# A retention layer with a GELU feed-forward layer on one core: the steps behind the 540th in another order, some of them on other engines

## The chip, the cores and the metric

The kernel runs on one core of a Trainium2 chip. Five engines work side by side: TensorE (PE in the profile; its weight loads PEld) multiplies matrices, VectorE (DVE), ScalarE (ACT) and GpSimd (POOL) work on elements, and SyncE (SP) issues DMA transfers. Each engine runs its own instructions in the order in which the program gives them, and waits for the others by semaphores. The metric is the device time of one execution in microseconds (us).

## The reference

```python
scores = scale * np.matmul(q, k.transpose(0, 1, 3, 2))      # q, k, v: 8 x 8 heads x 576 x 64
gamma = 1.0 - 2.0 ** (-5.0 - np.arange(H, dtype=np.float32))
Dmat = np.where(rel >= 0, gamma[:, None, None] ** rel[None, :, :], 0.0)
ret = scores * Dmat[None, :, :, :]
x = np.matmul(ret, v)                                       # then (b, s, h * d): 4608 x 512
h = x @ w_in                                                # 512 x 2048
g = 0.5 * h * (1.0 + np.tanh(c * (h + 0.044715 * h * h * h)))
out = g @ w_out                                             # 2048 x 512
```

Scores are decayed by the distance of two positions, with no softmax, so that the sum over earlier positions can be carried on as a state of 64 x 64 for each head.

## The kernel before

**Units and token blocks.** The 8 batches of 576 rows are cut into 40 units (u = 0 to 39), five for a batch: four of 128 rows and a tail of 64. The 4608 tokens of the second layer are cut into nine blocks (t = 0 to 8) of 512. The attention of a unit writes its columns of `xT`, a ring of three token blocks; a token block can begin when the units that cover it are done.

**The order is written out.** `ORDER` is a string of some 1370 steps. A loop at the end of the kernel takes them one by one and calls the function that the letter names; nothing reorders them later, so each engine's queue is the list, thinned to that engine's steps. Steps of different engines may overtake each other where their data allow. The last field of many steps names the engine: `v` VectorE, `a` ScalarE, `g` GpSimd; `q` without a letter is on VectorE.

**Steps of a unit u.** `L,u,n` loads q, k or v (n = 0, 1, 2) from SP into a page; a page is free again when the cast that reads it is done. `q,u` scales q by its decay to float16, `k,u` casts k, `v,u` scales v. `D,u` has a DMA on SP's queue transpose q and k. `B,u,w` is TensorE's work for the scores and the new state of unit u, and for the output of the unit before it, w (lines 550 to 595). `m,u` masks the scores, `a,u,h` adds to the state in float32 for either half h, `o` decays it, `z,u,h` makes its float16 copy in two instructions of 64 rows, and `x,u` moves the output into `xT`.

**Steps of a token block t.** Up to block 4 the first product is plain: `N,t,..` and `M` (line 790), with the gelu in `F` and `G`. For blocks 5 to 8 it is done with seven products of half size in place of eight: `s,t,i` makes four sums of blocks of `xT` (float16, in SBUF, in the area named `pages`), and `A,t,g,i` are the seven products of weight group g (line 1001). Their order in a group is 1, 6 and 2, 7 and 5, 4, 3: products 1, 6, 7 and 4 share one PSUM bank, 2, 5 and 3 the other, and `l,t,g,i` takes the partial results out (`l` 0 to 2 copy, 3 to 5 add). `f,t,g,i` is the gelu of a quarter. The second product is done in this way for most blocks: `H,t,pr,i` makes the sums of the gelu's output for a pair of 128 tokens (pr = 0 or 1; `ssum` in the profile, float16 in SBUF), `W,t,pr,i` are the seven products (line 904), and `V,t,pr,i` takes them out of PSUM into `u` and `ost`; `S,t,n` stores an `ost` from SP. `H,..,5` makes the two sums 1 and 3 in one instruction of 2048 columns, `H,..,1` and `H,..,3` make them one by one:

```python
if i == 5:
    a21, a11 = blk_a(t, pr, 1, 0), blk_a(t, pr, 0, 0)
    ...
    return combine(eng, s[4], a21.unsqueeze(1).to_broadcast([128, 2, HK, 128]), both, ALU.subtract)
```

All sums go through `combine` (line 850), copies and casts through `copy_on` (lines 284 and 286), the scalings of q and v through `times` (line 441):

```python
def combine(eng, out, a, b, op):
    (nc.vector if eng == "v" else nc.gpsimd).tensor_tensor(out=out, in0=a, in1=b, op=op)
```

**Buffers.** `ost` is a ring of four, so the `V` that begins the fifth waits for the store of the first; `qk16`, `v16` and the transposed `T` are rings of four units; `sz` (of `z`) is a ring of six. From unit 26 on nine pages are left for loads, since the sums of `w_in` and `xT` lie in the others. `i` and `j` steps cast a staged weight where there is one; here all weights are loaded and cast by DMAs on GpSimd's queue at the start, and these steps issue nothing.

Of the kernel before, what the change touches and what calls it, by code (L numbers as in the profile page):

```python
# [59 lines left out]
z,20,1,a B,21,20 F,3,14,1 F,3,2,1 L,26,0 N,4,4,0 a,21,0 L,24,1 W,3,1,1 m,21 U,3,0 V,3,0,0,a a,21,1  # L60
# [5 lines left out]
v,26,g V,3,1,3,a N,4,6,0 v,24,g k,27,a W,3,0,5 k,26,v z,23,1,g D,24 F,4,6,1 F,4,6,0 B,24,23 L,30,1
x,23 D,25 M,4,1 G,4,1 m,24 S,2,0 N,4,10,0 W,3,1,4 V,3,1,5,v B,25,24 D,26 W,3,0,2 a,25,0,g S,2,3
F,4,10,0 z,25,0,g V,3,0,4,v a,25,1 M,4,3 x,24 k,30,a W,3,0,3 D,27 G,4,3 m,25 H,4,0,5,v B,26,25
N,4,8,1 a,26,0 x,25 S,2,2 a,26,1 m,26 H,3,1,4,v v,27,g L,31,1 z,25,1,a F,4,8,1 k,31,a W,3,1,5
N,4,4,1 H,4,0,2,v z,26,0,g F,4,4,1 N,4,10,1 V,3,1,4,v B,27,26 N,4,14,1 L,28,0 W,3,1,3 V,3,0,6,v  # L70
L,29,0 L,28,1 o,26,1 x,26 s,5,1 F,4,10,1 V,3,0,2,a F,4,14,1 W,3,1,2 A,5,0,1 s,5,2 W,4,0,1 L,29,1
# [1047 lines left out]
```

## Time and profile before

| what | value |
|---|---|
| median of three runs | 294.59 us (294.44 to 296.1) |
| profiled execution, whole | 295.5 us |
| its span | 293.8 us |
| TensorE busy | 280.0 us (95%) |
| VectorE busy | 225.7 us (77%) |
| ScalarE busy | 166.6 us (57%) |
| GpSimd busy | 95.7 us (33%) |
| granted TensorE clock | 1.00 throughout |
| DMA | 49.77 MB, mean 169 GB/s |

The span is what the profiler saw of the one execution; 1.7 us lie around it. A row of a group gives the line, the engine, the operation, the tiles written and read, the shape, the count, the busy time in us with the mean of one in ns, and then the idle time of the engine ahead of it and what ended it. A row of the timeline gives start and duration in us, and in brackets the engine's idle time before. Rows of the trace are matched to steps by their order on each engine, which is the list's.

### The profile page before, as it was taken

What the parts mean: (1) busy time and instruction counts of PE and PEld (TensorE: products, weight loads), DVE (VectorE), ACT (ScalarE), POOL (GpSimd) and SP (SyncE); (2) the same over time, 40 slices, a digit from 0 to 9 for tenths busy, and PEclk for the clock granted to TensorE, in tenths of its full rate; (3) what the DMA queues carried; (4) which work ended last, traced back from release to release, by engine and by line L of the source; (5) the groups of instructions that cost most, each with busy time, mean ns of one, the idle gap of its engine ahead of it and who ended that gap; (6) DMA issues with size and microseconds to landing.
All of it is one profiled execution on the core that took longest, in us unless ns stands there. A gap on an engine that the chain in (4) does not pass through costs nothing.

```text
span 293.8 us, 9639 instructions
## 1 busy us (share of the span) xinstructions
PE 280.0 (95%) x4042; PEld 233.0 (79%) x4042; DVE 225.7 (77%) x446; ACT 166.6 (57%) x325; POOL 95.7 (33%) x157
## 2 busy tenths in 40 slices
PE   7697999999999999999999899999999999999995
PEld 2366767788888888888888778878887788888874
DVE  6684874986976798748758798899988989985841
ACT  2464763456655534656457558578576697655510
POOL 7841791202531321434643534644313301000000
PEclk9999999999999999999999999999999999999999
DMA  6999999949989979999998979997948430110112
GB/s 159 312 247 212 310 203 207 186 94 225 169 207 233 198 168 196 222 206 159 248 206 196 184 163 197 197 188 193 181 87 187 109 126 2 38 74 36 74 71 108
DMA packets 136428, 49.77 MB, mean 169 GB/s; under 512 B 118209, under 2 KB 130881, under 8 KB 136385
## 3 DMA queue, kind: packets, MB, share of 16 engines
q1 hardware_dynamic: 132032, 44.97, 70.6%
q0 software_dynamic: 4352, 4.20, 8.5%
q8 instruction: 31, 0.51, 0.8%
q14 instruction: 13, 0.10, 0.1%
HBM read 36.70 MB, written 9.44 MB: 157 GB/s over the span
## 4 chain that ended last, share of the span: by engine, by line
PE 77%; DVE 11%; DMA 5%; issue 2%; ACT 1%; SPq 1%; POOL 1%; DVEq 0%; POOLq 0%; ACTq 0%
PE bank L904 29%; PE bank L790 21%; PE bank L1001 14%; PE bank L816 4%; DMA w_in_sb<-in_moe_w_in_dram 3%; DVE ssum L850 2%; DVE pages L850 2%; PE sk L574 2%; PE x L550 2%; DMA pages<-in_q_dram 2%; PE sk L584 1%; PE x L595 1%; PE bank L1031 1%; DVE sz L764 1%; DVE hc L850 1%
## 5 line engine op out<-in xcount | busy, mean ns | idle before, releaser
L790 PE MATMUL bank<-xT,w_in_sb 128*128 128x256 f16 (+1 forms) x608 | 79.0, 279 | 1.8 <-ACT xT L607 0.9
L798 ACT ACTIVATE gT<-bank 128x512 f16<-128x512 f32 x80 | 47.0, 597 | 39.5 <-PE bank L790 39.2
L790 PEld LDWEIGHTS <-w_in_sb 128*128 128x128 f16 x608 | 57.5, 98 | 13.2 <-DMA w_in_sb<-in_moe_w_in_dram 2.5
L904 PEld LDWEIGHTS <-ssum 128*128 128x128 f16 x512 | 49.8, 98 | 6.8 <-DVE ssum L850 0.9
L904 PE MATMUL bank<-tsum,ssum 128*128 128x256 f16 x384 | 49.3, 273 | 0.3 <-DVE ssum L850 0.3
L904 PEld LDWEIGHTS <-gT 128*128 128x128 f16 x384 | 37.0, 98 | 4.4
L441 POOL TENSOR_TENSOR v<-pages,dec 128x512 f16<-128x512 f32 (+1 forms) x24 | 24.2, 1010 | 48.5 <-DMA pages<-in_v_dram 26.6
L286 POOL CAST sz<-s 64x256 f16<-64x256 f32 x36 | 17.3, 479 | 62.1 <-DVE s L746 51.6
L904 PE MATMUL bank<-w_out_sb,gT 128*128 128x256 f16 x256 | 32.9, 273 | 0.0
L1001 PEld LDWEIGHTS <-pages 128*128 128x128 f16 x256 | 24.2, 98 | 7.1 <-issue 2.9
L1001 PE MATMUL bank<-pages 128*128 128x256 f16 x192 | 27.9, 273 | 1.9 <-DVE pages L850 1.3
L722 DVE TENSOR_TENSOR ret<-sk,mask 128x512 f16<-128x512 f32 (+1 forms) x32 | 19.8, 618 | 9.8 <-PE sk L584 5.2
L850 DVE TENSOR_TENSOR ost<-u,bank 128x256 f32<-128x256 f32 x48 | 19.4, 416 | 9.5 <-PE bank L904 9.3
L850 DVE TENSOR_TENSOR ssum<-gT,ssum 128x1024 f16<-128x1024 f16 x32 | 24.0, 754 | 0.1
L284 ACT COPY hc<-bank 128x512 f32<-128x512 f32 x27 | 15.8, 586 | 14.1 <-PE bank L1001 13.8
L850 DVE TENSOR_TENSOR ssum<-gT 128x2048 f16<-128x2048 f16 (+1 forms) x20 | 21.3, 1063 | 2.7 <-ACT gT L798 2.1
L850 DVE TENSOR_TENSOR hc<-hc,bank 128x512 f32<-128x512 f32 x29 | 19.8, 684 | 4.0 <-PE bank L1001 3.8
L1001 PEld LDWEIGHTS <-w_in_sb 128*128 128x128 f16 x192 | 18.6, 98 | 2.9 <-DVE pages L850 0.6
L441 POOL TENSOR_TENSOR qk<-pages,dec 128x512 f16<-128x512 f32 (+1 forms) x16 | 17.1, 1070 | 9.7 <-DMA pages<-in_q_dram 4.8
L746 DVE TENSOR_TENSOR s<-s,sk 128x256 f32<-128x256 f32 x36 | 15.0, 416 | 5.8 <-PE sk L584 4.5
L1001 PE MATMUL bank<-xT,w_in_sb 128*128 128x256 f16 x128 | 19.2, 273 | 0.0
L1019 ACT ACTIVATE gT<-hc 128x512 f16<-128x512 f32 x29 | 17.8, 630 | 2.0 <-DVE hc L850 2.0
(117 smaller groups left out, 445.9 us busy)
## 6 DMA issues: line engine op xcount, KB each, us to landing
out_dram<-ost SPq DMA_DIRECT2D x35, 256.0 KB, 2.6
pages<-in_q_dram SPq DMA_DIRECT2D x32, 256.0 KB, 5.1
pages<-in_k_dram SPq DMA_DIRECT2D x24, 256.0 KB, 4.4
pages<-in_v_dram SPq DMA_DIRECT2D x24, 256.0 KB, 4.4
pages<-in_v_dram SPq DMA_DIRECT2D x4, 512.0 KB, 12.5
pages<-in_k_dram SPq DMA_DIRECT2D x4, 512.0 KB, 6.9
w_in_sb<-in_moe_w_in_dram POOLq DMA_DIRECT2D x8, 256.0 KB, 10.2
w_out_sb<-in_moe_w_out_dram POOLq DMA_DIRECT2D x8, 256.0 KB, 7.9
```

The source lines that it names most:

```text
L284: nc.scalar.copy(out=o, in_=i)
L286: (nc.vector if eng == "v" else nc.gpsimd).tensor_copy(out=o, in_=i)
L441: eng.tensor_tensor(out=out, in0=pages[:, page_of[s["u"], i], 0:n], in1=dec[:, i // 2, s["j"], 0:n].unsqueeze(2).to_broadcast([128, n, D]) ...
L722: nc.vector.tensor_tensor(out=ret[:, :, 0:n], in0=now["two"][:, :, 0, 0:n], in1=mask.unsqueeze(1).unsqueeze(1).to_broadcast([128, 2, n, G] ...
L746: nc.vector.tensor_tensor(out=s32, in0=state[0], in1=kv, op=ALU.add)
L790: nc.tensor.matmul(hps[:, i, :], w_in_sb[:, ct, 128 * (fc + i) : 128 * (fc + i) + 128], xT[:, ct, TB * t % XR + lo : TB * t % XR + hi], st ...
L798: nc.scalar.activation(out=gTs[t][:, fc : fc + TB // (hi - lo), lo:hi], in_=h.pop((t, fc, lo)), func=AF.Gelu_apprx_tanh, bias=0.0, scale=1.0,)
L816: nc.tensor.matmul(ops[t, tcc], gTs[t][:, ft, 128 * tcc : 128 * tcc + 128], w_out_sb[:, ft, :], start=(ft == 0), stop=(ft == NFC - 1),)
L850: (nc.vector if eng == "v" else nc.gpsimd).tensor_tensor(out=out, in0=a, in1=b, op=op)
L904: nc.tensor.matmul(p["ps", bank][:, HN * col : HN * col + HN], a[:, k], b[:, k], start=(k == 0 and fresh), stop=(k == HK - 1), skip_group_ ...
L1001: nc.tensor.matmul(p["ps", bank][:, n], w[:, c, 128 * n : 128 * n + 128], x[:, c], start=(n == 0 and c == 0 and i in (1, 2, 5)), stop=(c = ...
L1019: nc.scalar.activation(out=gTs[t][:, f : f + 2, o : o + 256], in_=p["ps", 0] if i == 0 else p["c", i], func=AF.Gelu_apprx_tanh, bias=0.0, ...
```

## The change

`ORDER` is the only thing that differs. The first 551 steps of the string are the same; the 819 behind them stand in a new order. The work is the same but for how three pairs of sums are made: `H,6,0,5` and `H,7,0,5` are taken apart into `H,..,1` and `H,..,3`, and `H,7,1,1` and `H,7,1,3` are put together as `H,7,1,5`. Engines change for nine steps `k`, 17 `z`, six `q`, four `v`, 17 `V` and seven `l`; the totals of the engines stay close (steps `k`: ScalarE 16 for 13, GpSimd 12 for 13, VectorE 8 for 10; `q`: VectorE 20 for 18; `v`: VectorE 9 for 11). The sums `s` and `H` stay on VectorE and stand at other places among the steps of GpSimd. The parts of the diff that are spoken of below:

```diff
-D,21 m,19 N,3,0,1 L,22,2 F,3,12,1 B,20,19 V,2,1,4,v V,2,1,2,a F,3,0,1 k,25,v x,19 k,23,g m,20 L,25,2
+D,21 m,19 N,3,0,1 L,22,2 F,3,12,1 B,20,19 V,2,1,4,v k,25,v V,2,1,2,a F,3,0,1 x,19 k,23,g m,20 L,25,2
...
-A,5,0,2 H,4,1,5,v s,5,3 L,28,2 z,26,1,a W,4,0,2 A,5,0,7 l,5,0,3,v q,28 s,5,4 L,29,2 L,30,2 A,5,0,5
-l,5,0,2,a W,4,0,6 A,5,0,4 W,4,0,5 D,29 l,5,0,4,v V,4,0,1,a q,30,g A,5,0,3 m,27 f,5,0,0 H,4,1,2,v
-v,28,g z,27,0,g A,5,1,1 l,5,1,0,a l,5,0,5,v W,4,0,7 f,5,0,3 D,28 H,4,1,4,v a,27,1 V,4,0,3,a A,5,1,2
-A,5,1,6 l,5,1,3,v B,28,27 a,28,0 l,5,1,1,a z,27,1,v L,33,2 A,5,1,5 j,6,v A,5,1,7 W,4,0,4 q,31,g
...
-z,31,0,v S,3,2 W,4,1,4 l,5,3,3,v m,31 L,34,2 L,35,0 f,5,2,3 s,6,3 A,5,3,5 l,5,3,2,a A,5,3,4
-l,5,3,4,v s,6,1 q,32,g D,32 f,5,3,1 f,5,3,0 s,6,2 W,4,1,3 V,4,1,5,a v,33,g A,5,3,3 i,4,v f,5,2,2
...
-l,6,2,3,v V,5,1,5,v B,35,34 H,5,1,4,v m,35 f,6,2,1 A,6,2,5 A,6,2,4 l,6,2,4,v f,6,2,0 W,5,1,5 q,36
-A,6,2,3 L,39,2 f,6,1,3 A,6,3,1 a,35,0 l,6,2,5,v z,35,0,v D,36 l,6,3,0,a W,5,1,2 V,5,0,4,v v,36,g
...
-V,5,0,6,v l,6,3,4,v V,5,0,2,a s,7,1 f,6,3,0 A,6,3,3 s,7,3 W,5,1,3 z,35,1,g l,6,3,5,v A,7,0,1 s,7,2
-k,38,a l,7,0,0,a q,37,g W,6,0,1 A,7,0,6 V,6,0,0,a V,5,1,6,v l,7,0,1,a A,7,0,2 W,6,0,2 H,6,0,5,v
-f,6,3,3 a,36,0 A,7,0,7 l,7,0,2,a f,6,3,2 l,7,0,3,v A,7,0,5 s,7,4 W,6,0,5 k,37,v f,7,0,1 H,6,0,2,v
...
-l,7,3,5,v A,8,0,2 S,6,3 s,8,3 H,7,0,2,v A,8,0,7 V,7,0,0,a l,8,0,3,v W,7,0,6 l,8,0,2,a f,8,0,1
...
-l,8,0,4,v V,7,0,3,a H,7,1,3,v A,8,0,3 W,7,1,1 l,8,1,0,a A,8,1,6 l,8,0,5,v W,7,0,4 l,8,1,1,v A,8,1,2
-H,7,1,1,v A,8,1,7 f,8,0,2 l,8,1,3,v V,7,1,0,a V,7,0,5,a l,8,1,2,a S,6,2 H,7,1,2,v f,8,0,3 W,7,0,5
...
+N,4,10,1 L,30,2 s,5,1 F,4,14,1 H,4,0,4,v F,4,10,1 A,5,0,1 V,3,1,6,v L,29,1 W,4,0,1 a,27,0 A,5,0,2
+l,5,0,0,a L,28,2 z,27,0,a s,5,2 V,4,0,0,v A,5,0,6 l,5,0,3,v l,5,0,1,a S,3,1 W,4,0,6 A,5,0,7 s,5,4
+A,5,0,5 q,28,g V,3,1,2,a W,4,0,2 f,5,0,1 V,4,0,1,v l,5,0,2,a l,5,0,4,v H,4,1,5,v A,5,0,4 k,29,g
+v,28,g f,5,0,0 a,27,1 D,28 W,4,0,5 q,31,g L,35,1 k,30,g A,5,0,3 A,5,1,1 l,5,1,0,a V,4,0,2,a W,4,0,7
...
+a,28,0 l,5,1,2,a A,5,1,5 D,29 W,4,0,4 L,32,0 A,5,1,4 f,5,1,1 L,31,1 z,27,1,g D,30 V,4,0,4,v z,28,0,g
...
+l,5,2,0,a W,4,0,3 k,31,a W,4,1,1 l,5,1,5,v A,5,2,6 S,4,1 A,5,2,2 v,30,g H,4,1,2,v x,28 B,30,29
...
+A,5,3,7 k,33,a A,5,3,5 V,4,1,4,v W,4,1,2 L,34,2 a,31,0 l,5,3,2,a V,4,1,5,a A,5,3,4 W,4,1,3 s,6,1
+l,5,3,4,v f,5,3,1 s,6,2 s,6,3 v,33,g D,32 A,5,3,3 L,36,2 s,6,4 a,31,1 f,5,3,0 H,5,0,1,v L,36,1
+A,6,0,1 S,3,2 f,5,2,3 o,31,1 l,5,3,5,v v,32,g z,31,0,g W,5,0,1 L,34,1 V,5,0,0,v f,5,2,2 l,6,0,0,a
...
+l,6,1,5,v z,33,0,v q,36,g L,38,1 W,5,0,4 x,32 l,6,2,0,a f,6,1,1 j,6,v A,6,2,2 l,6,2,3,v A,6,2,6
+z,33,1,g l,6,2,1,v k,38,v V,5,0,5,a L,35,2 W,5,1,4 B,34,33 V,5,1,5,v q,35,g A,6,2,7 H,5,0,4,v
+W,5,0,5 v,35,g k,35,a A,6,2,5 l,6,2,2,a l,6,2,4,v x,33 L,37,0 q,37 A,6,2,4 L,39,2 W,5,0,2 m,34
+V,5,0,4,v A,6,2,3 D,35 f,6,2,0 D,36 f,6,2,2 L,37,1 A,6,3,1 f,6,1,3 L,38,0 B,35,34 l,6,2,5,v
+H,5,1,4,v W,5,0,3 v,37,g l,6,3,0,a f,6,1,2 A,6,3,2 A,6,3,6 a,35,0 W,5,1,5 z,35,0,g l,6,3,3,v x,34
...
+W,5,1,2 V,5,0,6,v l,6,3,2,a A,6,3,4 x,35 S,4,2 W,5,1,3 q,38,g a,36,0 l,6,3,4,v V,5,1,2,a L,38,2
+s,7,1 f,6,3,1 V,5,1,6,v S,5,2 f,6,3,0 A,6,3,3 A,7,0,1 l,6,3,5,v s,7,2 H,6,0,1,v k,37,a s,7,3
+l,7,0,0,a W,6,0,1 A,7,0,2 f,6,3,2 l,7,0,3,v s,7,4 A,7,0,6 V,6,0,0,v W,6,0,5 H,6,0,3,v H,6,0,2,v
+f,6,3,3 l,7,0,1,a A,7,0,7 a,36,1 l,7,0,2,a A,7,0,5 l,7,0,4,v W,6,0,2 m,36 A,7,0,4 W,6,0,6 A,7,0,3
+f,7,0,1 V,6,0,1,v f,7,0,0 z,36,0,g f,7,0,2 A,7,1,1 q,39,g l,7,0,5,v W,6,0,7 l,7,1,0,a z,35,1,a
...
+x,36 W,6,0,4 l,7,1,3,v A,7,1,5 l,7,1,2,a v,38,g V,6,0,5,a H,6,1,5,v a,37,0 S,5,3 l,7,1,4,v A,7,1,4
...
+H,7,0,1,v V,6,1,5,a W,7,0,1 l,7,3,5,v l,8,0,1,a V,7,0,0,a A,8,0,2 A,8,0,7 s,8,4 l,8,0,2,a f,7,3,3
+H,7,0,2,v l,8,0,3,v f,7,3,2 W,7,0,6 A,8,0,4 f,8,0,0 V,6,1,6,v A,8,0,5 V,7,0,1,v W,7,0,7 A,8,1,1
+H,7,0,4,v l,8,0,4,v H,7,1,5,v V,7,0,3,v A,8,0,3 f,8,0,1 l,8,0,5,v W,7,1,1 l,8,1,0,a A,8,1,6
...
+A,8,1,5 A,8,1,4 H,7,1,2,v V,7,0,4,v l,8,1,4,v W,7,1,6 f,8,1,0 A,8,1,3 f,8,0,2 j,5,g V,7,1,1,v
```

More of the change, by code (lines that the diff above doesn't have):

```diff
@@ L57 @@
 N,3,6,1 z,18,0,g B,19,18 F,3,6,1 W,2,1,4 D,20 H,2,1,4,v V,2,1,5,v S,1,2 L,21,2 x,18 N,3,12,1 L,25,1
[L58 removed]
+D,21 m,19 N,3,0,1 L,22,2 F,3,12,1 B,20,19 V,2,1,4,v k,25,v V,2,1,2,a F,3,0,1 x,19 k,23,g m,20 L,25,2
 N,3,14,1 a,20,0,g a,20,1 U,4,0 W,2,1,3 v,22,v v,21,g V,2,1,6,v N,3,2,1 i,6,a z,20,0,a W,3,0,1
[L60 removed]
+z,20,1,a B,21,20 F,3,14,1 F,3,2,1 L,26,0 N,4,4,0 a,21,0 L,24,1 m,21 U,3,0 W,3,1,1 V,3,0,0,a a,21,1
@@ L66 @@
[L66 to L71, printed above, removed]
@@ L125 @@
-V,8,0,6,v e,8,2,v S,8,0 P,0 E,0,v S,8,2 Q,2 Q,0 P,1 E,1,a j,0,a i,1,a Q,1
+o,21,1 v,23,g W,3,0,6 V,3,0,1,v z,21,0,g q,26,g x,20 N,4,14,0 H,3,1,5,v B,22,21 q,24 L,25,0
+H,3,1,2,v N,4,12,0 W,3,0,7 a,22,0 V,3,1,0,a a,22,1 L,27,0 S,2,1 z,21,1,g x,21 F,4,14,0 N,4,12,1
+W,3,1,6 m,22 F,4,12,0 F,4,12,1 z,22,0,g V,3,1,1,v M,4,0 B,23,22 G,4,0 L,26,2 V,3,0,3,v W,3,0,4
+k,24,g L,30,0 q,25 a,23,0 L,27,1 q,27,g m,23 z,22,1,v V,3,0,5,a z,23,0,v M,4,1 k,27,g x,22 v,24,g
+N,4,6,0 W,3,0,5 k,26,a a,23,1 z,23,1,v F,4,6,0 W,3,0,2 W,3,1,7 V,3,1,3,v G,4,1 D,24 L,29,0 v,25,g
@@ new lines @@
+V,3,0,4,v B,24,23 M,4,2 D,25 m,24 N,4,10,0 x,23 B,25,24 i,4,a D,26 S,2,0 v,27,g H,3,1,4,v W,3,0,3
+G,4,2 M,4,3 S,2,3 v,26,g W,3,1,4 a,25,0,g a,25,1 L,30,1 F,4,10,0 m,25 x,24 z,25,0,a D,27 L,28,1
+G,4,3 H,4,0,5,v B,26,25 V,3,1,5,a L,29,2 a,26,0 N,4,4,1 V,3,0,6,v z,26,0,g W,3,1,5 q,29 m,26
+z,25,1,a a,26,1 L,28,0 N,4,8,1 x,25 S,2,2 F,4,4,1 F,4,8,1 k,28,a N,4,6,1 F,4,6,1 H,4,0,2,v B,27,26
+N,4,14,1 o,26,1 z,26,1,a W,3,1,2 m,27 V,3,1,4,v q,30 V,3,0,2,a L,33,0 W,3,1,3 x,26 s,5,3 L,31,0
+N,4,10,1 L,30,2 s,5,1 F,4,14,1 H,4,0,4,v F,4,10,1 A,5,0,1 V,3,1,6,v L,29,1 W,4,0,1 a,27,0 A,5,0,2
@@ new lines @@
+i,7,a l,8,3,1,v S,6,3 W,7,0,2 l,8,3,3,v f,8,2,3 f,8,2,2 A,8,3,7 j,7,g S,7,1 V,7,0,2,a l,8,3,2,v
+W,7,1,3 A,8,3,5 V,7,0,6,v i,3,a f,8,3,1 A,8,3,4 V,7,1,6,v W,8,0,1 l,8,3,4,v W,7,1,2 A,8,3,3 S,7,3
+f,8,3,0 S,7,0 V,8,0,0,a H,8,0,1,v H,8,0,2,v W,8,0,6 V,7,1,2,a W,8,0,5 V,8,0,1,v f,8,3,2 W,8,0,2
+l,8,3,5,v W,8,0,7 H,8,0,4,v f,8,3,3 V,8,0,3,v P,2 W,8,0,4 V,8,0,2,a V,8,0,4,v V,8,0,5,v W,8,0,3
+S,8,1 O,8,8 O,8,9 S,7,2 O,8,10 O,8,11 E,2,a V,8,0,6,v e,8,2,v S,8,0 P,0 E,0,v S,8,2 Q,2 Q,0 P,1
+E,1,a j,0,a i,1,a Q,1
```

68 lines of the change are left out of this document (25 added, 43 removed).

## The prediction

> **What bounds the kernel now.** I read the page's head first, then the busy time by stage, then what TensorE waited for behind the first changed step, then the stretches of the timeline around those waits.
>
> ```profile
> span 293.8 us, 9639 instructions
> PE 280.0 (95%) x4042; PEld 233.0 (79%) x4042; DVE 225.7 (77%) x446; ACT 166.6 (57%) x325; POOL 95.7 (33%) x157
> ...
> 124.10:164.70 40.60, 40.60 (x722) 34.72 (x721) 27.77 (x54) 23.37 (x48) 18.31 (x25) 1.00 1.06 206
> 164.70:194.60 29.90, 28.11 (x410) 24.20 (x408) 26.57 (x49) 19.38 (x39) 15.68 (x21) 1.00 0.85 179
> 194.60:223.80 29.20, 28.45 (x466) 25.27 (x465) 26.42 (x55) 20.81 (x40) 7.36 (x12) 1.00 0.85 173
> 223.80:251.50 27.70, 27.07 (x378) 23.80 (x377) 25.67 (x51) 20.20 (x40) 4.76 (x7) 1.00 0.31 82
> 251.50:290.70 39.20, 38.67 (x350) 32.61 (x348) 25.64 (x47) 17.79 (x35) 0.00 (x0) 1.00 0.18 70
> ```
>
> TensorE bounds it. The columns of the stretches are the length, then the busy time of TensorE, its weight loads, VectorE, ScalarE and GpSimd. The first changed step runs at about 124 us; the other borders are the first matmuls of `A,5`, `A,6`, `A,7` and `A,8`, and the last matmul. The order of matmuls within a stage changes, their number does not, so the change can only move TensorE's idle time: 0 in the first stretch, then 1.79, 0.75, 0.63 and 0.53, together **3.70 us**. That is the ceiling of the gain. VectorE is the second bound: it is busy 26.57 of 29.90 us behind `A,5`, the share at which a late VectorE step has no room to be made up.
>
> ```profile
> PE bank L1001 <- DVE pages L850: 1.6, 3, 0.8
> PE bank L1001 <- DVE hc L850: 0.8, 2, 0.7
> PE bank L1001 <- ACT hc L284: 0.5, 2, 0.3
> PE bank L904 <- DVE ssum L850: 0.3, 1, 0.3
> PE sk L574 <- DVE ret L722: 0.3, 1, 0.3
> ```
>
> TensorE's named waits behind 124 us come to 3.5 us (total, times, longest); all but 0.5 are for VectorE, most for sums that lie in SBUF (`pages` holds the sums of `s`, and those of `l` in part; `ssum` those of `H`). Why these are late shows where GpSimd runs beside them:
>
> ```profile
> 167.13 1.19 POOL L441 TENSOR_TENSOR v<-pages,dec 128x512 f16<-128x512 f32 x1 [2.08 <-DMA pages<-in_v_dram]
> 167.34 1.26 DVE L850 TENSOR_TENSOR pages<-xT 128x512 f16<-128x512 f16 x1
> ...
> 168.66 1.19 PE L1001 MATMUL bank<-pages 128*128 128x256 f16 x8 [0.77 <-DVE pages L850]
> ...
> 169.40 1.36 POOL L441 TENSOR_TENSOR qk<-pages,dec 128x512 f16<-128x512 f32 x1
> ...
> 169.78 1.26 DVE L850 TENSOR_TENSOR pages<-xT,pages 128x512 f16<-128x512 f16 x1
> ...
> 189.12 1.04 POOL L441 TENSOR_TENSOR qk<-pages,dec 128x512 f16<-128x512 f32 x1
> ...
> 189.58 1.78 DVE L286 CAST sz<-s 64x256 f16<-64x256 f32 x2
> ...
> 227.89 1.10 POOL L441 TENSOR_TENSOR v<-pages,dec 128x512 f16<-128x512 f32 x1
> ...
> 228.01 1.52 DVE L850 TENSOR_TENSOR ssum<-gT,ssum 128x1024 f16<-128x1024 f16 x1
> ```
>
> `s,5,3` (167.34) and `s,5,4` (169.78) take 1.26 us each: each starts 0.2 to 0.4 us into a GpSimd step and ends about 0.3 us behind that step's end. `z,31,0` (189.58) and `H,6,0,2` (228.01) show the same. Without a GpSimd step beside them the same forms are shorter; the first five rows are from 249.9 us on, where GpSimd is idle, the last three from 161 to 230 us:
>
> ```profile
> L850 DVE TENSOR_TENSOR ssum<-gT,ssum 128x1024 f16<-128x1024 f16 x6 | 4.1, 687 | 0.1
> L850 DVE TENSOR_TENSOR ssum<-gT 128x1024 f16<-128x1024 f16 x4 | 2.7, 686 | 0.4 <-ACT gT L1019 0.4
> L850 DVE TENSOR_TENSOR ssum<-gT 128x2048 f16<-128x2048 f16 x1 | 1.2, 1215 | 0.0
> L850 DVE TENSOR_TENSOR pages<-xT,pages 128x512 f16<-128x512 f16 x2 | 0.8, 424 | 0.1
> L850 DVE TENSOR_TENSOR pages<-xT 128x512 f16<-128x512 f16 x2 | 0.8, 418 | 0.0
> ...
> L850 DVE TENSOR_TENSOR ssum<-gT,ssum 128x1024 f16<-128x1024 f16 x8 | 6.3, 788 | 0.0
> L850 DVE TENSOR_TENSOR pages<-xT,pages 128x512 f16<-128x512 f16 x6 | 4.0, 674 | 0.0
> L850 DVE TENSOR_TENSOR pages<-xT 128x512 f16<-128x512 f16 x6 | 3.8, 648 | 0.8 <-ACT xT L614 0.8
> ```
>
> So the sums lose 8 x 0.10 + 6 x 0.25 + 6 x 0.23 = 3.7 us of VectorE's time to GpSimd in that stretch. At `A,5` it shows directly: `A,5,0,7` waits 0.77 us for `s,5,3`, and `A,5,0,4` for `s,5,4`.
>
> **The change, part by part.** (1) *Where the sums stand.* The two GpSimd steps that hold `s,5,3` and `s,5,4` are `v,28` (167.13) and `q,31` (169.40). In the new list GpSimd has 12 steps between `A,5,0,1` and `A,6,0,1` where it had 17 (15.68 us, so some 4.6 us less), and `z,27,1,g`, which must wait for VectorE's `a,27,1`, stands ahead of `v,30`; `s,5,2` and `s,5,4` stand ahead of `a,27,1`, so GpSimd should wait then. In exchange GpSimd has 16 steps behind `A,6` (10 before) and 6 behind `A,7` (6). How well this is met is not in the trace: GpSimd does not keep to its place in the list. `v,28,g` stands behind `A,5,0,3` there, yet ran at 167.13, ahead of `A,5,0,7` at 168.66, since its data were there. By my hand count of the new queue (`q,28`, `k,29`, `v,28`, `q,31`, `k,30`, each as its load lands), GpSimd is busy from about 162.5 to 166 on the clock of this trace. That still meets `s,5,3`, `s,5,1` and `H,4,0,4`, which have 3 us until TensorE asks for them, and should leave `s,5,2` and `s,5,4` free.
>
> Bounds for `A,5`: between 0 and the whole 1.79 us. I take -0.8: of the some 1.2 us at 167.9 to 171.1 two thirds. (2) *`z,31,0` goes to GpSimd* (1.78 us on VectorE at 189.58, just ahead of the wait for `s,6,3`): of the remaining 0.6 us, -0.4, bounds 0 and -0.6. (3) *Behind `A,6`*: VectorE has 45 steps for 49, GpSimd 16 for 10: more meetings, less load. -0.1, bounds -0.75 and +0.5 (two collisions of 0.25 at these rows). (4) *Behind `A,7`*: `H,6,0,5` is taken apart into `H,6,0,1` and `H,6,0,3`: 2 x 0.686 - 1.215 = +0.16 us of VectorE, and it needs `f,6,3,0` and `f,6,3,1` alone ahead of `W,6,0,5`. `H,6,0,2` now stands where GpSimd has `v,38,g` next, which must wait for `B,37,36`; but `z,36,0,g` and `q,39,g` come free beside `s,7,2` and `s,7,3`. -0.3 of 0.63, bounds +0.2 and -0.63. (5) *Behind `A,8`* GpSimd is idle in both; `H,7,0,5` is taken apart (+0.16) and `H,7,1,5` takes the place of `H,7,1,1` and `H,7,1,3` (-0.16). -0.1, bounds +0.3 and -0.5. (6) *Other engines.* Nine casts of k, 17 of z, six of q, four of v, 17 copies `V` and seven `l` change engine:
>
> ```profile
> L284 ACT CAST qk<-pages 128x512 f16<-128x512 f32 x5 | 3.1, 620 | 0.0
> L441 DVE TENSOR_TENSOR qk<-pages,dec 128x512 f16<-128x512 f32 x3 | 2.1, 700 | 0.0
> ```
>
> ScalarE gets 16 k casts for 13, at 0.62, and one `z` and one `l` more, one `V` less, some 2.9 us more in all; it is busy 19.4 of 29.9, 20.8 of 29.2 and 20.2 of 27.7 us, so its idle time hides them, and where that cover is gone a gelu is later by one cast, 0.6 us. VectorE's whole load behind 124 us falls by about 1 us. `i` and `j` steps do nothing here, since the weights come in by another way. The first stretch gets five VectorE steps more on 27.77 of 40.60 us: 0, or 0.6 if a gelu is late.
>
> (7) *Loads and transposes, the term against the change.* SP's queue holds loads, transposes `D` and stores `S` in list order. Landing times (median us from issue):
>
> ```profile
> pages<-in_q_dram SPq DMA_DIRECT2D x32, 256.0 KB, 5.1
> ...
> qkT<-qk SPq DMA_TRANSPOSE x31, 3.8
> ...
> 165.74 5.42 SPq L504 DMA_TRANSPOSE qkT<-qk  x2
> ...
> 215.97 1.26 SPq L504 DMA_TRANSPOSE qkT<-qk  x1
> ...
> 219.64 0.28 PE L550 MATMUL x<-qkT,sz 128*128 128x64 f16 x4
> ```
>
> The first transposes are `D,29` and `D,28`: `D,29` stands behind `W,4,0,5` in the list and issues 2.9 us ahead of `A,5,0,7`, so SP runs ahead too. The last two rows are `D,36` and `B,36,35`, the tightest pair now, 3.67 us apart. The new list has `z,33,1,g`, `q,35,g` and `k,35,a` just ahead of `D,35`, and only `A,6,2,5`, `A,6,2,4`, `W,5,0,2`, `A,6,2,3` and `A,6,3,1` between `k,35,a` and `B,35,34`. Eight matmuls of a `W` take 0.87 us at full rate, four of an `A` 0.44 (the chain's row below): 4 x 0.44 + 0.87 = 2.6 us, less the cast's own 0.6, against 3.8 for the transpose.
>
> ```profile
> 172.58 0.87 PE bank L1001 x8
> 173.45 0.87 PE bank L904 x8
> ```
>
>  Unless `k,35,a` runs early (ScalarE has little ahead of it there) `B,35,34` waits: bounds 0 and 3.8 - 2.0 = 1.8; I take +0.3, nearer the low end, since SP's row at 165.74 shows that it runs ahead of the list where its data allow. `D,36`, `L,37,1`, `L,38,0`, `S,5,1`, `L,39,0` and `S,4,2` queue behind `D,35`; `V,5,1,2` needs the buffer that `S,4,2` frees, on VectorE, ahead of `s,7,1`: bounds 0 and 1.0, +0.1. `q,37` now on VectorE stands directly behind the issue of its load; SP must be some 5 us ahead, 2.9 at the row above: 0, or 1.0; +0.1.
>
> Sum: -0.8 - 0.4 - 0.1 - 0.3 - 0.1 + 0.3 + 0.1 + 0.1 = **-1.2 us**. The profiled execution took 295.5 us with its span of 293.8, so 294.3 for it; it lies 0.9 over the median of the runs, 294.59, and from that the sum gives **293.4 us**.
>
> The Trainium skill (SBUF — State Buffer, Who interferes with whom) says that a VectorE instruction with two SBUF inputs and a GpSimd instruction that reads SBUF exclude each other, and that the order of issue decides which of them is held. The rows at 167.34 and 228.01 agree. By that rule a sum put ahead of a GpSimd step holds that step instead, so the loss may only change sides; the second rival below is its price here.
>
> **The rivals.** *Nearly all of the idle time goes* (-3.1): sums, `z,31,0` and `H,6,0,2` all free of GpSimd, and SP in time. For it: all but 0.5 of 3.5 us of waits name VectorE. Against: some waits have other causes (`hc`, 0.7), and GpSimd's place in the list is not kept. 291.5 us.
>
> *The collisions only move.* GpSimd has 50 steps behind 124 us in both lists and runs them as soon as data land, among as many sums; what `A,5` gains, `A,6` with its 16 steps loses: +-0 with 0.5 either side, 294.6 us. For it: GpSimd's run ahead at 167.13. Against: the stage behind `A,5` had the most GpSimd work (15.68 us) and the most idle time (1.79).
>
> *Slower: the transpose `D,35` comes late.* It decides if `q,35,g` or `k,35,a` ends less than 3.8 us ahead of `B,35,34`. Full price 1.8, and as SP is then late for `S,4,2` and `q,37`'s load 1.0 + 1.0 more on VectorE; with half of the gains of (1) to (5) kept (-0.9), +2.9: 297.5 us. For it: `z,33,1,g` is the long form and waits for `a,33,1` directly ahead of `q,35`. Against: `k,35`'s load is early.
>
> **How the numbers follow.** Forecast 293.4: 0.46; nearly all goes, 291.5: 0.15; collisions only move, 294.6: 0.25; transpose late, 297.5: 0.14. The forecast's own range is 292.1 to 294.4. The range reaches from 3.6 us below (all idle time) to the slower rival: **291.0 to 297.5**. A run of this kernel can be told from no change at about 1%, 2.9 us: faster by that, below 291.6, is half of the first rival and a rest of the forecast, 0.14; slower, above 297.5, is half of the last rival and some unseen mishap, 0.1; the rest, 0.76.
>
> **What would show each step.** Right: TensorE's idle time behind `A,5` falls from 1.79 to about 0.6, and `s,5,4` takes 0.42; `H,6,0,2` takes 0.69; the `pages<-xT` sums' mean falls from 0.65 towards 0.42. Wrong: `pages` and `ssum` waits of TensorE unchanged in sum, or a wait of `B,35,34`'s scores (line 584) for a DMA, or VectorE idle ahead of `V,5,1,2` or `q,37`.

## The result, and the profile after

The changed kernel takes **293.22 us** (median of eight runs, 292.47 to 294.44), the kernel before 294.84 beside it (eight runs, 294.11 to 296.83): ratio 0.9941, 95% interval 0.9917 to 0.9966, a gain of 1.6 us. Below, "after" is the changed kernel; its line numbers are one higher than those of before. The head of its page, and the busy time by stage over the same steps as in the prediction (length, then TensorE, its weight loads, VectorE, ScalarE, GpSimd, the granted clock):

```profile
span 291.3 us, 9650 instructions
...
124.10:164.60 40.50, 39.99 (x715) 34.02 (x713) 28.56 (x58) 23.39 (x49) 15.61 (x20) 1.00 1.05 200
164.60:193.00 28.40, 27.49 (x411) 24.62 (x410) 24.28 (x51) 19.87 (x40) 12.99 (x17) 1.00 1.07 201
193.00:221.30 28.30, 28.28 (x467) 25.25 (x465) 23.62 (x46) 21.94 (x44) 14.22 (x20) 1.00 0.77 178
221.30:248.60 27.30, 27.14 (x378) 23.77 (x376) 24.74 (x54) 19.11 (x38) 3.42 (x4) 1.00 0.29 79
248.60:287.90 39.30, 38.66 (x350) 32.59 (x348) 25.05 (x47) 18.68 (x38) 0.00 (x0) 1.00 0.16 63
```

TensorE's idle time (length less its busy time) is 0.51, 0.91, 0.02, 0.16 and 0.64 us, together 2.24, where it was 3.70. The stages behind `A,5`, `A,6` and `A,7` are 1.5, 0.9 and 0.4 us shorter, the first stretch has a wait that it did not have before, and behind `A,8` nothing changes. Behind `A,5` the length falls by more than the idle time (1.5 against 0.9 us); the part on the prediction comes back to this. What TensorE still waits for from 124 us on (total, times, longest), all of it; the first two rows are new places to wait:

```profile
PE sk L585 <- DVE ret L723: 0.7, 1, 0.7
PE bank L905 <- DVE ost L851: 0.5, 1, 0.5
PE bank L1002 <- ACT pages L285: 0.3, 1, 0.3
PE bank L1002 <- ACT hc L285: 0.3, 1, 0.3
PE bank L1002 <- DVE pages L851: 0.2, 1, 0.2
```

The sums `s` now take what they took without GpSimd beside them. Groups of VectorE from 161 to 230 us (count, busy time, mean ns of one):

```profile
L851 DVE TENSOR_TENSOR ssum<-gT,ssum 128x1024 f16<-128x1024 f16 x9 | 7.4, 822 | 0.0
...
L851 DVE TENSOR_TENSOR pages<-xT,pages 128x512 f16<-128x512 f16 x6 | 2.5, 416 | 0.0
L851 DVE TENSOR_TENSOR pages<-xT 128x512 f16<-128x512 f16 x6 | 2.5, 422 | 0.5 <-PE bank L1002 0.5
```

The means of the twelve sums `s` fell from 674 and 648 ns to 416 and 422; those of `H` into `ssum` did not fall (788 to 822). GpSimd's timeline shows why the sums `s,5` are free, and VectorE's shows what else happens there (start, duration, then the idle time ahead and what ended it):

```profile
161.86 1.04 POOL L442 TENSOR_TENSOR qk<-pages,dec 128x512 f16<-128x512 f32 x1 [3.94 <-DMA pages<-in_q_dram]
168.55 0.40 POOL L287 CAST qk<-pages 128x256 f16<-128x256 f32 x1 [5.64 <-DMA pages<-in_k_dram]
169.64 2.01 POOL L442 TENSOR_TENSOR v<-pages,dec 128x512 f16<-128x512 f32 x1 [0.69 <-DMA pages<-in_v_dram]
```

```profile
162.40 0.42 DVE L851 TENSOR_TENSOR ost<-u,bank 128x256 f32<-128x256 f32 x1 [1.24 <-PE bank L905]
...
165.64 0.41 DVE L851 TENSOR_TENSOR pages<-xT,pages 128x512 f16<-128x512 f16 x1
...
167.24 0.42 DVE L851 TENSOR_TENSOR pages<-xT,pages 128x512 f16<-128x512 f16 x1
...
169.53 1.22 DVE L851 TENSOR_TENSOR ssum<-gT 128x2048 f16<-128x2048 f16 x1
...
176.06 0.42 DVE L851 TENSOR_TENSOR ost<-u,bank 128x256 f32<-128x256 f32 x1 [1.42 <-DMA out_dram<-ost]
...
225.78 0.69 DVE L851 TENSOR_TENSOR ssum<-gT,ssum 128x1024 f16<-128x1024 f16 x1
```

After `q,28` (161.86) GpSimd stands still for 5.64 us, because the next in its queue, `k,29`, waits for its load until 168.55; `s,5,2` (165.64) and `s,5,4` (167.24) run in that pause. In before the same step `k,29` had begun at 162.67; SP issued its load at 159.57 us there and at 165.56 here. This is no accident of one execution: in the profiles of the three variants of after below, `k,29` began at 168.76, 168.90 and 169.58. The collision that comes then has the other sign: `H,4,1,5` (169.53) was first and keeps its 1.22 us, and `v,28` (169.64) takes 2.01 us where 1.04 is usual. No wait of TensorE names a step of GpSimd. The Trainium skill (SBUF — State Buffer, Who interferes with whom) says that the one that issues first blocks the other; both signs are in these traces, `s,5,4` at 1.26 us before and `v,28` at 2.01 us after.

The two new waits are both steps that stand behind something they do not need. `V,3,1,4` (162.40) stands behind `W,3,1,2` in the new list and waited for its end; `W,3,1,3` needs the bank that it frees (0.5 us). `V,4,0,4` (176.06) waited 1.42 us for the store `S,3,3` to free its buffer, `a,28,1` and `m,28` are queued behind it, and the scores of `B,29,28` wait for `m,28` (0.7 us).

### The profile page after: what moved, and what is told of

It is laid out like the page before. It is cut to its first block, busy times and chain, and to the rows that moved or that the text cites. A ratio compares the mean times of both kernels' runs of the same rounds, so it can differ in the third digit from the quotient of the medians.

```text
span 291.3 us, 9650 instructions
## 1 busy us (share of the span) xinstructions
PE 278.8 (96%) x4042; PEld 233.2 (80%) x4042; DVE 222.3 (76%) x445; ACT 168.3 (58%) x330; POOL 96.5 (33%) x154
## 4 chain that ended last, share of the span: by engine, by line
PE 83%; DMA 7%; DVE 2%; SPq 2%; POOL 2%; ACT 1%; issue 1%; ACTq 0%; POOLq 0%; DVEq 0%
PE bank L905 32%; PE bank L791 23%; PE bank L1002 16%; DMA w_in_sb<-in_moe_w_in_dram 4%; PE bank L817 4%; PE sk L575 2%; PE x L551 2%; DMA pages<-in_q_dram 2%; DMA out_dram<-ost 2%; PE sk L585 1%; PE x L596 1%; PE bank L1032 1%; POOL w_in_sb L256 1%; SPq L239 1%; POOL wide L458 1%; DVE ssum L851 1%
## 5 line engine op out<-in xcount | busy, mean ns | idle before, releaser
L442 POOL TENSOR_TENSOR v<-pages,dec 128x512 f16<-128x512 f32 (+1 forms) x26 | 28.5, 1105 | 59.7 <-DMA pages<-in_v_dram 30.0
L442 POOL TENSOR_TENSOR qk<-pages,dec 128x512 f16<-128x512 f32 (+1 forms) x14 | 14.8, 1055 | 10.7 <-DMA pages<-in_q_dram 8.5
```

The lines of the kernel that those rows point to most:

```text
L442: eng.tensor_tensor(out=out, in0=pages[:, page_of[s["u"], i], 0:n], in1=dec[:, i // 2, s["j"], 0:n].unsqueeze(2).to_broadcast([128, n, D]) ...
```

## The experiments

Each of these runs was timed beside before on the same chip, in three groups; the medians of before were 294.91 in the first (letters, order, both short kernels), 295.53 in the second (s ahead, q,31 early, z,31, two moves) and 295.66 us in the third (s free, l ahead, both, short again). The time of one execution of before scatters by 0.9 to 1.4% within a group, and a part of that lies ahead of the changed steps: in the profiled executions of the kernels that leave that part alone, the first matmul behind the 540th step starts at 128.97 to 130.27 us. So each profile is also read by stages, which are not touched by it. One profile of each kernel is still one execution: where two lists agree, the stage behind `A,5` differs by 0.3 us (before, and l ahead) and the first stretch by up to 0.8 us (before, and both). Lengths in us from border to border (first matmul behind the 540th step, `A,5`, `A,6`, `A,7`, `A,8`, last matmul), each from the stretches of its timeline:

| kernel | first stretch | `A,5` | `A,6` | `A,7` | `A,8` | sum | ratio to before, 95% interval |
|---|---|---|---|---|---|---|---|
| before | 34.98 | 29.96 | 29.19 | 27.71 | 39.16 | 161.00 | |
| after | 35.65 | 28.37 | 28.29 | 27.33 | 39.24 | 158.88 | 0.9941, 0.9917 to 0.9966 |
| letters alone | 34.98 | 29.97 | 30.40 | 28.82 | 41.63 | 165.80 | 1.0216, 1.0183 to 1.0248 |
| order alone | 37.02 | 30.41 | 30.28 | 29.10 | 39.60 | 166.41 | 1.0191, 1.0156 to 1.0225 |
| before, short GpSimd | 34.97 | 27.75 | 29.39 | 26.83 | 39.17 | 158.11 | 0.9989, 0.9971 to 1.0007 |
| after, short GpSimd | 35.67 | 27.48 | 28.20 | 27.05 | 39.24 | 157.64 | 0.9986, 0.9965 to 1.0008 |
| before, short again | 34.98 | 27.65 | 29.06 | 26.83 | 39.16 | 157.68 | 0.9920, 0.9886 to 0.9954 |
| before, s ahead | 35.53 | 30.23 | 29.18 | 27.55 | 39.16 | 161.65 | 1.0012, 0.9991 to 1.0033 |
| before, s free | 34.99 | 29.49 | 29.19 | 27.54 | 39.17 | 160.38 | 0.9968, 0.9942 to 0.9995 |
| before, l ahead | 34.98 | 30.24 | 28.35 | 27.72 | 39.17 | 160.46 | 0.9993, 0.9966 to 1.0019 |
| before, both | 35.74 | 28.87 | 28.77 | 27.94 | 39.16 | 160.48 | 0.9964, 0.9940 to 0.9988 |
| after, q,31 early | 36.44 | 27.83 | 28.27 | 27.05 | 39.23 | 158.82 | 0.9952, 0.9928 to 0.9977 |
| after, z,31 on VectorE | 36.74 | 28.00 | 28.28 | 27.33 | 39.24 | 159.59 | 0.9938, 0.9913 to 0.9964 |
| after, two moves | 35.36 | 28.10 | 28.28 | 27.05 | 39.23 | 158.02 | 0.9932, 0.9907 to 0.9956 |

**Letters or order alone.** First theory: GpSimd's meetings with VectorE's sums are what before loses, and the new places avoid them. First rival: the new distribution over engines gains by itself.

```diff
 (letters alone: before's list)
-z,31,0,v S,3,2 W,4,1,4 l,5,3,3,v m,31
+z,31,0,g S,3,2 W,4,1,4 l,5,3,3,v m,31
 ... (60 such letters; order alone: the same 60 the other way in after's list)
```

> The list of before, with the engine letters of after for its q, k, v, z, V and l steps behind the 540th (60 steps change engine, none its place; S, L, D and the matmuls stay). Theory: the gain of 1.6 us (before 294.84, after 293.22) comes from where GpSimd's steps stand beside VectorE's sums, so letters alone bring little: z,31,0 leaves VectorE (-0.4), s,5,3 or s,5,4 still take over 0.8 us. 0 to -0.6 us against before. First rival: the new distribution over engines brings the gain by itself: -1.2 to -1.8 us, with s,5,3 and s,5,4 near 0.42 us.

> The list of after with the engine letters of before for the same steps (60 letters back). Theory: the order carries most of the gain: -0.8 to -1.4 us against before, s,5,1 to s,5,4 at 0.42 us each, the wait at z,31,0 back. First rival (engines alone): 0 +- 0.4 us against before, as the order has nothing to give.

Measured: 301.18 and 300.55 us, 6.3 and 5.6 us slower than before. Both expectations missed, in sign too. Either half alone breaks the list. My reading, argued from the waits and not tested step by step, is that a step that changes engine stands in that engine's queue behind other work than the list was made for. Two of VectorE's waits from 160 to 280 us in the kernel with the letters alone (total, times, longest); in before the first is 3.8 us, and the second, a copy that waits for a gelu of ScalarE, isn't there:

```profile
DVE hc L850 <- PE bank L1001: 5.7, 7, 1.8
...
DVE hc L286 <- ACT gT L1019: 2.0, 1, 2.0
```

So neither half can be credited with the gain, and what follows changes single steps.

**GpSimd's steps cut short.** The collisions are taken away as far as the program allows: from unit 23 on, GpSimd's `q`, `k`, `v` and `z` steps do one head where they did eight. They leave out the other heads, and their length falls to a third and not to an eighth: the `v` steps take 361 ns each where the long ones took 1084.

```diff
 def times(s, eng, out, i):
     n = s["n"]
+    if eng is nc.gpsimd and s["u"] >= 23:
+        n, out = 1, out[:, 0:1]
 ... (the casts k, and z, in the same way; tiles of qk16 and v16 allocated once)
```

> Before, with GpSimd's q, k, v and z steps of units 23 and later cut to one head of eight (or one of a half's four pairs); the other heads of these tiles keep stale values, so the output is not the reference's. The qk and v tiles are allocated once and set to zero. Collisions of VectorE's sums with GpSimd become eight times shorter. Theory: TensorE's idle time behind A,5 falls by the collisions' share; s,5,3 and s,5,4 at 0.42 to 0.55 us; 1.0 to 1.8 us faster than before. Rival (the sums' collisions are not what TensorE waits for): within 0.4 us of before.

> After, with the same cut of GpSimd's steps as in the kernel of the same call. Theory: where there are no collisions the two lists are worth the same, but for the two waits that only after has (m,28 1.0 us, W,3,1,3 0.7 us): 0 to 1.5 us slower than the shortened before. Rival: the list itself is better, whatever GpSimd does: 1.2 to 1.8 us faster than the shortened before.

> Before, with GpSimd's q, k, v and z steps from unit 23 on cut to one head as in before_short (the other heads keep stale values, the output is not the reference's), without the eight settings to zero that made that kernel's first 130 us some 1.8 us longer. Theory: with collisions all but gone TensorE loses nothing behind A,5 and A,7 (1.79 and 0.63 us in before), 0.75 behind A,6: 2.0 to 2.6 us less than before (ratio 0.991 to 0.993). Rival: within 0.8 us of before.

In whole time the first two came out as before (294.40 and 294.53 us), but their changed part begins at 131.5 and 133.2 us, as setting the tiles to zero delays the first units; by stages they gain 2.9 and 3.4 us. Without these settings the same cut of before takes **292.51 us**, 2.4 less by the ratio, as expected. Its stages `A,5` to `A,7`, and all that TensorE still waits for between 160 and 249 us (this kernel's lines stand eleven further down than before's):

```profile
164.06:191.71 27.65, 27.65 (x410) 24.40 (x408) 23.55 (x50) 18.87 (x39) 5.95 (x21) 1.00 0.91 195
191.71:220.77 29.06, 28.39 (x466) 25.22 (x464) 25.28 (x55) 21.07 (x41) 3.34 (x12) 1.00 0.81 178
220.77:247.60 26.83, 26.83 (x378) 23.88 (x376) 24.69 (x51) 20.19 (x40) 2.21 (x7) 1.00 0.29 81
```

```profile
PE bank L1012 <- DVE hc L861: 0.7, 1, 0.7
PE bank L1012 <- ACT hc L289: 0.3, 1, 0.3
```

Behind `A,5` and `A,7` TensorE has no idle time left: the 1.79 and 0.63 us of before were GpSimd's doing, all of it, and the stages are 2.31 and 0.88 us shorter. The cut also makes GpSimd's results ready sooner, so this run alone does not tell collisions from late results; but no wait of TensorE or VectorE behind 160 us in before names a step of GpSimd, and the sums `s` now take 434 and 418 ns. Behind `A,6` 0.67 of 0.75 us stay, so that stage loses its time otherwise. And with GpSimd cut short the two lists are worth about the same in sum, after at 157.64, before at 157.68 and 158.11 us: after's first stretch is 0.7 us longer and its stage `A,6` 0.9 to 1.2 shorter. The rival (after 1.2 to 1.8 us faster) falls; the first theory (0 to 1.5 slower) holds by the whole times, 294.53 against 294.40 us, and misses by 0 to 0.5 us by the stages.

**Two sums moved.** If positions are what counts, moving only `s,5,3` and `s,5,4` should pay.

```diff
-A,5,0,2 H,4,1,5,v s,5,3 L,28,2 z,26,1,a W,4,0,2 A,5,0,7 l,5,0,3,v q,28 s,5,4 L,29,2
+A,5,0,2 s,5,3 s,5,4 H,4,1,5,v L,28,2 z,26,1,a W,4,0,2 A,5,0,7 l,5,0,3,v q,28 L,29,2
```

> Before, with s,5,3 and s,5,4 moved ahead of H,4,1,5 in the list, nothing else: by the trace of before they then run at about 166.2 to 167.0 us, where GpSimd is idle between q,30 (end 165.05) and v,28 (167.13). Theory: both take 0.42 us instead of 1.26, TensorE's waits of 0.77 and 0.5 us behind A,5 go: -0.8 to -1.3 us against before. Rival (the waits at A,5 have another cause, or H,4,1,5 is now what is late): within 0.4 us of before.

Measured: 295.80 us, no change. The rows of GpSimd and of VectorE there:

```profile
166.84 1.04 POOL L441 TENSOR_TENSOR qk<-pages,dec 128x512 f16<-128x512 f32 x1 [1.96 <-DMA pages<-in_q_dram]
```

```profile
166.55 0.42 DVE L850 TENSOR_TENSOR pages<-xT 128x512 f16<-128x512 f16 x1
166.89 1.27 DVE L850 TENSOR_TENSOR pages<-xT,pages 128x512 f16<-128x512 f16 x1
```

`s,5,3` is free. `s,5,4` met `q,30`, which in before had ended at 165.05 and here waited for its load until 166.84: the list ahead of the moved sums is the same, but the load landed some 3 us later, of which 1.2 us is its later issue (160.23 in before, 161.47 here). So only one of the two sums was freed. (The second wait that the theory names is 0.37 us in before's trace; a wait of 0.49 us is another one, of `A,5,3,5`.) The second version also takes `q,30` out of the way:

```diff
 (besides the two sums)
-V,4,0,1,a q,30,g A,5,0,3 m,27 f,5,0,0 H,4,1,2,v v,28,g z,27,0,g A,5,1,1
+V,4,0,1,a A,5,0,3 m,27 f,5,0,0 H,4,1,2,v v,28,g z,27,0,g q,30,g A,5,1,1
```

> Before, with s,5,3 and s,5,4 ahead of H,4,1,5 as in the run s_ahead, and q,30 moved behind z,27,0, since q,30, whose load landed 3 us later there, met s,5,4. GpSimd then has nothing ready from the end of q,29 until v,28's load lands. Theory: s,5,3 and s,5,4 take 0.42 us each, TensorE idles 0.4 to 0.9 us behind A,5 instead of 1.8 to 2.2, and the time falls by 0.8 to 1.3 us (ratio 0.9955 to 0.997). Rival (the wait goes to H,4,1,5 or to a GpSimd step made late): within 0.4 us of before.

Measured: 294.60 us, 0.95 us less by the ratio (interval 0.15 to 1.7), as the theory has it. GpSimd, VectorE and TensorE:

```profile
167.82 1.04 POOL L441 TENSOR_TENSOR v<-pages,dec 128x512 f16<-128x512 f32 x1 [3.82 <-DMA pages<-in_v_dram]
```

```profile
165.93 0.42 DVE L850 TENSOR_TENSOR pages<-xT 128x512 f16<-128x512 f16 x1
166.27 0.42 DVE L850 TENSOR_TENSOR pages<-xT,pages 128x512 f16<-128x512 f16 x1
```

```profile
168.47 0.60 PE L1001 MATMUL bank<-pages 128*128 128x256 f16 x4 [0.42 <-DVE pages L850]
```

Both sums take 0.42 us, and a wait of 0.42 us is left, now for `l,5,0,3` behind the moved `H,4,1,5`: the rival has a part of it. The stage does not bear out the theory's size: its length fell by 0.5 us only and its idle time to 1.50 us, not to 0.4 to 0.9. A later collision was dearer in this execution (`z,31,0` beside GpSimd's `q,32` and `v,33`: 2.05 us where before had 1.78), and the wait behind it was 0.76 us where before had 0.49.

**The stage that had no collision.** Before's VectorE ahead of `A,6,3,3`, with the 0.7 us wait of the prediction's row for `hc`:

```profile
219.00 0.41 DVE L850 TENSOR_TENSOR ost<-u,bank 128x256 f32<-128x256 f32 x1
221.44 0.42 DVE L850 TENSOR_TENSOR ost<-u,bank 128x256 f32<-128x256 f32 x1 [2.03 <-PE bank L904]
221.78 0.68 DVE L850 TENSOR_TENSOR hc<-hc,bank 128x512 f32<-128x512 f32 x1
```

VectorE stands still for 2.03 us: `V,5,0,6` waits for the end of `W,5,0,2`, and `l,6,3,4`, which TensorE waits for, is queued behind it. After has `l,6,3,4` elsewhere.

```diff
-A,6,3,4 x,35 V,5,0,6,v l,6,3,4,v V,5,0,2,a
+A,6,3,4 x,35 l,6,3,4,v V,5,0,6,v V,5,0,2,a
```

> Before, with l,6,3,4 moved ahead of V,5,0,6, nothing else. In the trace of before VectorE stands idle from 219.4 to 221.4 us, because V,5,0,6 waits for W,5,0,2's end, and l,6,3,4, which is ready and for which A,6,3,3 waits 0.7 us, is queued behind it. Theory: the gain behind A,6 (0.73 us of TensorE's idle time) is this order and no collision: that stage's idle time falls from 0.75 to about 0.1 and the time by 0.6 to 0.8 us (ratio 0.997 to 0.998). Rival (collisions made VectorE late there): no change.

Measured: 295.00 us, no change. The stages `A,6` and `A,7`, and `l,6,3,4` there:

```profile
195.06:223.41 28.35, 28.28 (x466) 25.25 (x464) 26.25 (x55) 20.80 (x40) 7.37 (x12) 1.00 0.78 164
223.41:251.13 27.72, 27.07 (x378) 23.87 (x376) 25.78 (x51) 20.19 (x40) 4.96 (x7) 1.00 0.34 92
```

```profile
220.88 0.69 DVE L850 TENSOR_TENSOR hc<-hc,bank 128x512 f32<-128x512 f32 x1 [1.05 <-ACT hc L284]
```

The stage is 0.84 us shorter and its idle time 0.07 (0.02 in after): the cause of this stage's loss is shown. `l,6,3,4` was not ready all the time that VectorE stood still, as the expectation has it: even at the head of the queue it waits 1.05 us for a copy of ScalarE, and starts at 220.88 where before had 221.78. That is enough, since TensorE lost 0.67 us there. In whole time the gain is not seen: the interval runs from 1.0 us less to 0.6 more, so it holds the expected 0.7 and nothing at all alike; `A,5` happened to lose 0.28 us more in the profiled execution. With the other edit:

> Before, with both of these edits (three steps moved, one GpSimd step moved back). Theory: the two places add up to most of what the whole change gains: 1.4 to 2.1 us less than before (ratio 0.993 to 0.995), as after. Rival (the gain of after is spread over many steps): under half of it, 0 to 0.8 us.

Measured: 294.44 us, 1.1 us less by the ratio. That is under the 1.4 expected and over the rival's 0.8; after gains 1.7 by the ratio. The interval, 0.4 to 1.8 us, holds a part of both. By stages `A,5` (-1.1) and `A,6` (-0.4) gain; `A,7` loses 0.2, and the first stretch 0.8 ahead of all the edits.

**After, with single steps put back.**

```diff
 (q,31 early)
-A,5,0,4 k,29,g v,28,g f,5,0,0 a,27,1 D,28 W,4,0,5 q,31,g L,35,1
+A,5,0,4 q,31,g k,29,g v,28,g f,5,0,0 a,27,1 D,28 W,4,0,5 L,35,1
 (z,31,0 on VectorE)
-V,4,1,4,v W,4,1,2 L,34,2 a,31,0 l,5,3,2,a
+V,4,1,4,v W,4,1,2 L,34,2 a,31,0 z,31,0,v l,5,3,2,a
 ...
-v,32,g z,31,0,g W,5,0,1
+v,32,g W,5,0,1
```

> After, with q,31 moved ahead of k,29 in the list, so that GpSimd runs it at about 165.0 to 166.4 us, beside s,5,2 (165.64 in after), where GpSimd now waits for k,29's load. Theory: s,5,2 takes over 0.9 us instead of 0.41, VectorE is 0.5 to 0.9 us later, and A,5 loses 0.3 to 0.9 us against after (ratio to before about 0.997). Rival (collisions are hidden by VectorE's slack): as after, 0.994 to before.

> After, with z,31,0 back on VectorE, directly behind a,31,0 and ahead of the sums s,6,1 to s,6,4. Theory: it costs VectorE 0.9 to 1.8 us there and TensorE 0.4 us (bounds 0 to 0.6, as predicted) behind A,5. Rival (VectorE has room there): 0 against after.

Measured: 294.01 and 293.64 us, both as after. `q,31` did not start where it was meant to: it began at 168.23, inside `s,5,2` (168.05, 0.41 us), which was first, and ended as `s,5,4` (169.32, 0.41 us) began. Neither sum is longer, so this run says nothing of the price of a sum that comes second. `z,31,0` back on VectorE costs nothing:

```profile
191.04 0.79 DVE L286 CAST sz<-s 64x256 f16<-64x256 f32 x2
191.86 0.42 DVE L850 TENSOR_TENSOR pages<-xT 128x512 f16<-128x512 f16 x1
```

It takes 0.79 us where it took 1.78 in before. Most of the difference is GpSimd, which ran beside all of it in before and beside its first 0.3 us here (0.58 us for two such casts without GpSimd, as in the s free run at 186.19). TensorE has no wait between 189 and 194 us. This run has after's list up to 189 us, and in it `B,29,28` did not wait for `m,28`: that new wait of after is not in every execution.

**Two moves for after's new waits.**

```diff
-N,4,14,1 o,26,1 z,26,1,a W,3,1,2 m,27 V,3,1,4,v q,30
+N,4,14,1 o,26,1 z,26,1,a V,3,1,4,v W,3,1,2 m,27 q,30
 ...
-f,5,0,0 a,27,1 D,28 W,4,0,5 q,31,g ... A,5,1,6 l,5,1,1,a S,3,3
+f,5,0,0 a,27,1 D,28 S,3,3 W,4,0,5 q,31,g ... A,5,1,6 l,5,1,1,a
```

> After, with the store S,3,3 moved up directly behind D,28 and V,3,1,4 moved up ahead of W,3,1,2. Theory: the two waits that after has in the place of the old ones are of the list's making: the buffer of the output rows that V,4,0,4 waits for comes 2 us sooner (TensorE -1.0 us at 176 us), and W,3,1,3 finds its bank free (-0.7 us at 162 us): 291.3 to 291.9 us, 1.3 to 1.7 us less than after. Rival: TensorE's gain is given back within the same stages by VectorE, which is no earlier: 292.8 to 293.3 us.

Measured: 293.56 us, ratio 0.9932, not to be told from after's 0.9941. The theory's 1.3 to 1.7 us are missed; on the scale of after's group the ratio gives 292.8 us, the rival's number. Both waits are gone from its profile (`V,4,0,4` ran at 175.18 without one); what TensorE waits for from 129 to 249 us is a single row:

```profile
PE sk L585 <- DMA qkT<-qk: 0.3, 1, 0.3
```

By stages it is 0.9 us shorter than after's profile, and 1.6 shorter than the profile of after with `z,31,0` moved; in whole time that does not show. The rival's mechanism, a gain given back within the stages, is not seen either. With the waits of after differing from execution to execution, one profile of each cannot say how much of it stays. It is the shortest complete kernel by its changed part, not a proven gain over after.

## Why the prediction was right, and where it was not

The size and the sign hold: 293.4 us forecast, 293.22 measured, a gain of 1.6 where the sum of terms gave 1.2. Between the two profiles the changed part is 2.1 us shorter: 2.0 behind `A,5` and `A,7`, where the short GpSimd steps show that GpSimd was the whole loss, 0.9 behind `A,6`, where it was a queue, less 0.7 of the first stretch. The main mechanism, sums that lose time to GpSimd, was right. That the number came so close is in part luck: the sum missed 0.8 us of gain behind `A,6` and 0.7 us of loss in the first stretch, and these nearly cancel.

The premise that the change can only move TensorE's idle time, with 3.70 us as the ceiling, is too narrow. Idle time is counted from the end of the last matmul row, and rows overlap: eight matmuls of a product take 0.87 us in the chain, so one starts about every 0.11 us, while the row of one lasts 0.27. By an estimate from these two figures each wait costs some 0.16 us more than its idle time, and shorter ones do not show at all. With GpSimd cut short the changed part is 3.3 us shorter where the idle time of `A,5` to `A,7` fell by 2.5, and the 0.84 us of `l,6,3,4` come on top: by this estimate about 4.2 us were there to gain. Lengths of stages are the safer measure.

The terms, one by one, against the stages:

- **(1) The sums at `A,5`, -0.8.** Idle time 1.79 to 0.91; the stage is 1.59 us shorter, with the gain of (2) in it. That these sums lose to GpSimd, and that TensorE pays, is shown (GpSimd cut short: 0.00; s free: both at 0.42 us and 0.95 us less in whole time). The working of where they would come free was wrong. It had GpSimd busy from 162.5 to 166 and idle behind `z,27,1`; the trace has it idle from 162.9 to 168.55 because `k,29`'s load was issued late, which the prediction did not foresee: `s,5,2` and `s,5,4` came free as it said, for another reason. And 0.7 of the 0.91 us left is a new wait (`m,28`).
- **(2) `z,31,0` to GpSimd, -0.4.** Not supported. The wait that it stood ahead of is gone, but put back on VectorE it costs nothing, at 0.79 us. Dear was the meeting with GpSimd (1.78 us), not the engine. The wait was also misread: `A,5,3,5` waited for `l,5,3,3` (191.39), queued behind `z,31,0`, and `s,6,3` began only after it (192.60):

```profile
191.39 0.69 DVE L850 TENSOR_TENSOR pages<-pages,bank 128x512 f32<-128x512 f32 x1
192.13 0.60 PE L1001 MATMUL bank<-pages 128*128 128x256 f16 x4 [0.49 <-DVE pages L850]
192.60 0.95 DVE L850 TENSOR_TENSOR pages<-xT 128x512 f16<-128x512 f16 x1
```

- **(3) Behind `A,6`, -0.1.** Mis-sized: 0.75 to 0.02, -0.73. The term was taken from counts of steps. The row `hc L850: 0.8, 2, 0.7` was quoted and set aside as another cause; its longest wait, 0.67 us, was nearly all of this stage's loss, `l,6,3,4` behind `V,5,0,6`, and one move gets it (0.07 left).
- **(4) Behind `A,7`, -0.3.** 0.63 to 0.16; the stage is 0.38 us shorter. `H,6,0,2` takes 0.69 us (225.78), as said; with GpSimd cut short the stage's idle time is 0.00.
- **(5) Behind `A,8`, -0.1.** None: 0.53 to 0.64 by these borders.
- **(6) The first stretch, 0 or 0.6.** 0.51, by `V,3,1,4` behind `W,3,1,2`; no gelu was late. In the profiles of after and its three variants this stretch is 0.4 to 1.8 us longer than 34.98; in those of before and its four variants with full GpSimd steps 0 to 0.8.
- **(7) Loads and transposes, +0.5.** The transpose `D,35` (+0.3) was not late:

```profile
208.70 2.63 SPq L505 DMA_TRANSPOSE qkT<-qk  x2
```

```profile
214.13 0.30 PE L585 MATMUL sk<-qkT 64*64 64x64 f16 x16
```

Issued at 208.70, with the scores of `B,35,34` at 214.13: `q,35` and `k,35` ran ahead of the list. `V,5,1,2` and `q,37` did not wait for a DMA. A store that holds a buffer of `ost` did come late, the mechanism named for `S,4,2`, but a block earlier, at `S,3,3`, for 0.7 us of TensorE in that one profile. So the term's size was near and its place wrong.

Of the rivals, "the collisions only move" is half true: GpSimd now waits for VectorE (its eight long `v` steps take 1225 ns each from 161 to 230 us, seven took 1084 before), and no wait of TensorE names GpSimd. GpSimd's cost is not all gone, either: with its GpSimd steps cut short after's changed part is another 1.2 us shorter (158.88 and 157.64), 0.9 of it behind `A,5`, where the new wait for `m,28` lies.
